# First loads in another order, the values of two blocks in one set of transfers, the first weights in four transfers, and the scales of expert 0's weights from sums of absolutes on ACT

## The chip, the core and the metric

The kernel runs on one core of one Trainium2 chip. The metric is the device time of one execution in microseconds (us): the kernel before took 1921.61 us, the median of three runs (1919.76 to 1923.17). The profile is that of one execution which took 1919.81 us. Its span, from the first to the last instruction, is 1917.9 us, so 1.9 us of that execution lie around the span.

## The reference

Chunked attention with memory tokens gives a 3072 x 512 matrix. A mixture of eight experts works on it, and each expert's output is weighted by a doubly normalised matrix P.

```python
# attention: B=4, H=8, S=768, D=64; chunks of 32, context 16 left and 8 right, 8 memory tokens
for c in range(S // 32):
    k_full = concat(mem_k, k[:, :, max(0, 32*c - 16) : min(S, 32*c + 40)])
    v_full = concat(mem_v, v[:, :, same rows])
    a = softmax(q[:, :, 32*c : 32*c + 32] @ k_full.T / 8)
    out[:, :, 32*c : 32*c + 32] = a @ v_full
x = out.transpose(0, 2, 1, 3).reshape(3072, 512)
# experts: w_gate 512x8, w1 8x512x1024, w2 8x1024x512
P = exp(x @ w_gate - max); 8 times: rows of P to sum 1, columns of P to sum 1, P *= 3072 / 8
for e in range(8):
    y += P[:, e:e+1] * (relu(x @ w1[e]) @ w2[e])
```

## The kernel before

The tokens are cut into 24 blocks of 128 (six for each of the four batch entries) and into six units of 512 (four blocks), each made of two groups of 256. The attention makes a block at a time. Queries, keys and "extra" keys (`kx`: the keys after the block, and the memory keys) are loaded and turned on TensorE (`tq`, `tk`, `tx`), the scores (`sp`) are made in 64 small matmuls, VectorE takes the maximum and subtracts it, ScalarE takes the exponential, the weights are turned (`ta`), multiplied with the values (`xp`), divided by their sum (`rec`, `xq`) and turned into a column layout (`xt`, copied to `xg`).

The experts' matmuls are done in 16-bit pairs: a 32-bit operand is multiplied by a power of two, its upper part is rounded to 16 bits on ScalarE (line 513), and VectorE takes the rest (line 521). Three products of the parts stand for one 32-bit product. The power of two for an operand is found from its largest absolute value (`scales`, line 434): a maximum along each partition, a transpose of the 128 maxima on TensorE (`row_x`, `row_w`), a maximum of these, a bit mask that leaves the exponent, a matmul that spreads the result over the partitions (`sp_x`, `sp_w`), and a reciprocal. For the values of the attention the maxima of `v` serve as a bound of its output: `vmax` (line 974) is found for each of the first four blocks, of blocks 0 and 1 for the first group's scale, and of all four for the first unit's.

Expert 0 on the first unit is made as plain products, so that it can begin early: `pp` (line 2045) are its first layer's products for one group of 256 tokens, `yp` (line 2126) its second layer's. They need expert 0's `w1` in four pieces (`w1f`, loaded by lines 543 to 553 and split by `plain1`), its `w2` in four pieces (`w2f`, split by `plain2`), and the two scales. All later products (`px`, `py`, `pz`, `yx`, `yy`, `yz`, line 1598) use a seven-product scheme for 2 x 2 blocks.

The program is not written in the order in which it runs. Every step is a task with an engine, a cost, what it depends on and a priority, and `Plan.run` (line 164) plays the tasks against these costs and hands out the instructions of each engine in that order. Where the plan finds TensorE without work for more than 0.4 us, it lays filling matmuls there (`warm`, line 427), which compute nothing that is used. The order is fixed when the program is built: on the chip each engine takes its instructions in that order and waits where an input is missing. Loads and stores are issued by SP (SyncE's queue), some of the first by ACT (ScalarE's queue). The framework gives every transfer one of eight semaphores in turn (called DMAHW0 to 7 in the program), and a transfer is not issued before the transfer eight places earlier has landed.

The names and lines for what follows: `load_block` (q and k of a block), `load_extra` (kx), `load_values` with `go_v` (line 921, eight transfers of 56 KB for a block), `go_m` and `copy_m0` (lines 890 and 908, the memory values and their copies within the on-chip memory), `take_m` (line 913, the copy of finished value buffers on POOL for the next blocks), `load` and `most` (lines 549, 551 and 558), `fetch_first` and `first_hidden`. Of the ACT queue's order at the start one has to know that the value loads of line 921 stand on it ahead of ScalarE's first computation.

Of the kernel before, what the change touches and what calls it, by code (L numbers as in the profile page):

```python
# [23 lines left out]
ISSUE = 0.5  # L24
BEHIND = 5.0
FIRST = 2.0
MARGIN = 8.0
APART = 3.6
# [3 lines left out]
class Task:  # L32


    __slots__ = ("eng", "cost", "fn", "prio", "left", "ready", "end", "then", "takes", "frees", "n", "dma", "start", "many")
# [55 lines left out]
class Plan:  # L91
# [14 lines left out]
    def add(self, eng, cost, fn, deps=(), prio=0.0, bufs=(), takes=None, frees=None, dma=0.0, many=False):  # L106
# [3 lines left out]
        t.many = many  # L110
        if dma:
            t.cost = cost * ISSUE
# [51 lines left out]
    def run(self):  # L164
        clock = {e: 0.0 for e in self.ENGINES}
        waiting = {e: [] for e in self.ENGINES}
        able = {e: [] for e in self.ENGINES}
        dma = FIRST
# [4 lines left out]
        while left:  # L173
# [45 lines left out]
            for s in t.then:  # L219
# [14 lines left out]
def tile_chunked_attn_sinkhorn_moe(  # L234
# [83 lines left out]
    ones = one.broadcast_to([P, P])  # L318
    idle = ident.bitcast(BF16)
# [114 lines left out]
    def scales(part, s, u, name, deps, prio, pool=None):  # L434
# [20 lines left out]
        def inverse(a):  # L455
            nc.vector.tensor_scalar_mul(u, a, 2.0**-SHIFT)
# [74 lines left out]
    w1v = w1.rearrange("e (kt p) (fh fp f) -> e fp p kt fh f", p=P, fh=2, fp=FP)  # L531
    w2v = w2.rearrange("e (fh fp p) d -> e fp p fh d", fh=2, fp=FP)
# [3 lines left out]
    def load(e, fp, which, prio, ahead="", eng="SP", after=()):  # L536
        shape = [P, 2, KT, P] if which == 1 else [P, 2, DM]
# [8 lines left out]
        def go():  # L546
            if which == 1:
                for fh in range(2):
                    queue.dma_start(st.t[:, fh], w1v[e, fp, :, :, fh])
# [3 lines left out]
        return st, add(eng, 2 if which == 1 else 1, go, after, prio, [st], dma=2.1)  # L553

    def most(e, fp, which, st, deps, prio):
        def go():
            flat = st.t.rearrange("p a k f -> p (a k f)" if which == 1 else "p a d -> p (a d)")
# [10 lines left out]
    def scale_w(e, which, deps, prio, pool=None):  # L568
# [9 lines left out]
            pool,  # L578
        )
# [14 lines left out]
    def cut(e, fp, which, st, ld, prio):  # L594
# [12 lines left out]
        if which == 1:  # L607
            a11, a12 = lambda: st.t[:, 0, 0:2], lambda: st.t[:, 0, 2:4]
            a21, a22 = lambda: st.t[:, 1, 0:2], lambda: st.t[:, 1, 2:4]
# [25 lines left out]
        if which == 1:  # L635
# [3 lines left out]
                    lambda: st.t[:, 0],  # L639
# [21 lines left out]
        else:  # L661
            pieces = [(slice(2, 3), slice(0, 1), (0.5, 0.65)), (slice(4, 7), slice(1, 4), (0.9, 1.1))]
# [1665 lines left out]
```

## Time and profile before

| | us |
|---|---|
| median of three runs | 1921.61 |
| the profiled execution | 1919.81 |
| its span | 1917.9 |
| TensorE (PE) busy | 1903.2 |
| VectorE (DVE) busy | 1436.4 |
| ScalarE (ACT) busy | 1033.6 |
| GpSimd (POOL) busy | 524.4 |

TensorE is busy in nearly the whole span, and what counts is therefore how much of this is work that has to be done. A row of the stretches has the stretch, its length, the busy time of each engine with its number of instructions, the granted clock (1.00 is full), the DMA engines' busy share (it can come out over 1) and the rate in GB/s. A row of the timeline has a start, a length, the engine, line, operation, what it writes and reads, the number of instructions merged, and in brackets how long the engine had been idle and what ended that. SPq and ACTq are the two queues that issue transfers.

### The profile page before, as it was taken

Reading aid. Unit: us, or ns where it says so; the run is one execution under the profiler, and the core shown is the slowest. Engines: PE = TensorE matmul, PEld = TensorE weight load, DVE = VectorE, ACT = ScalarE, POOL = GpSimd, SP = SyncE. Lnnn points to the kernel's source line nnn. Section 1 sums busy time; section 2 is a strip of 40 time slices with the busy share of each in tenths; the row PEclk is TensorE's granted clock in tenths of the full one; section 3 lists DMA queues with packets and bytes.
Section 4 is the critical chain, followed back from the end, with each engine's and each line's share of the span. In section 5 each row is a group of like instructions: output and inputs, shape, how many; then the busy total and the mean of one; then the engine's idle time right before and its main releaser. Section 6 shows DMA issues by size and latency. Waiting matters only on the chain.

```text
span 1917.9 us, 47295 instructions
## 1 busy us (share of the span) xinstructions
PE 1903.2 (99%) x19616; PEld 1641.0 (86%) x19616; DVE 1436.4 (75%) x2396; ACT 1033.6 (54%) x2019; POOL 524.4 (27%) x549
## 2 busy tenths in 40 slices
PE   9999999999999999999999999999999999999999
PEld 7777676688888888888888888888888888888888
DVE  6776569778679866898668875898678885786565
ACT  4765565556456545646445554655555554564453
POOL 1220001544224221432124231342124232332112
PEclk9999999999999999999999999999999999999999
DMA  8678753453235342265214533245313732322321
GB/s 198 174 194 209 171 172 116 129 204 125 83 110 172 127 148 85 78 197 185 92 63 149 197 105 127 78 160 176 138 45 105 242 122 94 100 83 84 127 83 67
DMA packets 246791, 254.82 MB, mean 133 GB/s; under 512 B 113264, under 2 KB 180272, under 8 KB 242224
## 3 DMA queue, kind: packets, MB, share of 16 engines
q1 hardware_dynamic: 244452, 251.21, 41.2%
q8 instruction: 153, 2.51, 0.6%
q10 hardware_dynamic: 2124, 0.59, 0.2%
q14 instruction: 62, 0.51, 0.1%
HBM read 187.84 MB, written 63.44 MB: 131 GB/s over the span
## 4 chain that ended last, share of the span: by engine, by line
PE 96%; DMA 2%; DVE 1%; ACT 0%; issue 0%; SPq 0%; ACTq 0%; DVEq 0%
PE px L1598 26%; PE yx L1598 23%; PE pz L1598 13%; PE yz L1598 11%; PE py L1598 6%; PE yp L2126 6%; PE yy L1598 6%; DMA q<-in_q_dram 1%; PE xp L1137 1%; PE sp L1069 1%; PE pp L2045 1%; PE tq L1006 1%; PE tk L1010 0%; PE ta L1127 0%; PE xt L1178 0%; DVE w L521 0%
## 5 line engine op out<-in xcount | busy, mean ns | idle before, releaser
L1598 PEld LDWEIGHTS <-w 128*128 128x128 f16 x7896 | 771.4, 98 | 91.9 <-issue 0.6
L1598 PEld LDWEIGHTS <-h 128*128 128x128 f16 x7056 | 690.4, 98 | 81.4 <-issue 1.5
L1598 PE MATMUL px<-x,w 128*128 128x256 f16 x4512 | 549.1, 273 | 0.0
L1931 POOL TENSOR_TENSOR acc<-acc,y 128x256 f32<-128x256 f32 x252 | 267.5, 1068 | 862.1 <-ACT y L1906 842.7
L1598 PE MATMUL yx<-w,h 128*128 128x256 f16 x4032 | 467.5, 273 | 1.3 <-DVE acc L1941 1.3
L1657 ACT ACTIVATE q<-px 128x256 f32<-128x256 f32 x376 | 142.8, 381 | 294.2 <-PE px L1598 289.5
L1598 PE MATMUL pz<-x,w 128*128 128x256 f16 x2256 | 278.2, 273 | 0.0
L1598 PE MATMUL yz<-w,h 128*128 128x256 f16 x2016 | 233.8, 273 | 0.0
L1826 DVE TENSOR_TENSOR h<-ss,h 128x1024 f16<-128x1024 f32 x160 | 215.0, 1346 | 4.0 <-ACT h L1802 3.5
L1777 ACT ACTIVATE h<-c 128x768 f16<-128x768 f32 x168 | 140.8, 838 | 106.4 <-DVE c L1667 106.4
L1802 ACT CAST h<-ss 128x1024 f16<-128x1024 f32 x168 | 174.1, 1039 | 20.4 <-DVE ss L1766 19.6
L1766 DVE SCALAR_TENSOR_TENSOR ss<-c,ss 128x256 f32<-128x256 f32 x336 | 168.3, 501 | 8.2
L1810 DVE SCALAR_TENSOR_TENSOR h<-c,h 128x768 f16<-128x768 f32 x168 | 165.3, 984 | 9.2 <-ACT h L1777 9.1
L1667 DVE SCALAR_TENSOR_TENSOR c<-px,q 128x256 f32<-128x256 f32 x188 | 78.0, 422 | 103.2 <-PE px L1598 94.9
L1906 ACT ACTIVATE y<-yx,pscale 128x256 f32<-128x256 f32 x168 | 79.4, 473 | 114.8 <-PE yx L1598 110.6
L1598 PE MATMUL py<-x,w 128*128 128x256 f16 x1128 | 139.2, 273 | 0.0
L2126 PE MATMUL yp<-w,h 128*128 128x512 f16 x576 | 132.0, 379 | 0.0
L1667 DVE SCALAR_TENSOR_TENSOR c<-py,q 128x256 f32<-128x256 f32 x188 | 78.5, 422 | 60.2 <-PE py L1598 56.7
L1766 DVE SCALAR_TENSOR_TENSOR ss<-c,h 128x512 f32<-128x512 f32 x168 | 120.8, 719 | 3.1 <-ACT h L1754 3.0
L1598 PE MATMUL yy<-w,h 128*128 128x256 f16 x1008 | 116.9, 273 | 0.0
L2126 PEld LDWEIGHTS <-h 128*128 128x128 f16 x576 | 56.0, 98 | 57.9
L513 ACT ACTIVATE w<-ws,sw 128x1024 f16<-128x1024 f32 (+1 forms) x64 | 69.3, 1089 | 65.5 <-POOL ws L602 65.5
(158 smaller groups left out, 1773.0 us busy)
## 6 DMA issues: line engine op xcount, KB each, us to landing
x<-xkeep SPq DMA_DIRECT2D x28, 1792.0 KB
akeep<-acc SPq DMA_DIRECT2D x168, 256.0 KB
acc<-akeep SPq DMA_DIRECT2D x168, 256.0 KB
w1f<-in_moe_w_dram SPq DMA_DIRECT2D x72, 256.0 KB
w2f<-in_moe_w_dram SPq DMA_DIRECT2D x32, 512.0 KB
w1fm<-in_moe_w_dram SPq DMA_DIRECT2D x56, 256.0 KB
w2fm<-in_moe_w_dram SPq DMA_DIRECT2D x28, 512.0 KB
xkeep<-x SPq DMA_DIRECT2D x6, 1792.0 KB
```

What stands on the lines that cost most here:

```text
L513: lambda: nc.scalar.activation(dst(0), src(), AF.Copy, scale=s),
L1598: nc.tensor.matmul(dst.t, a, b, start=(not more and n == 0), stop=(n == end), skip_group_check=more,)
L1657: lambda: nc.scalar.activation(t.t, src.t, AF.Copy, scale=DOWN),
L1667: lambda: nc.vector.scalar_tensor_tensor(c.t[:, o], src.t, DOWN, q.t, op0=ALU.mult, op1=ALU.add),
L1766: lambda: nc.vector.scalar_tensor_tensor(dst(), src(), 0.0, other(), op0=ALU.max, op1=op),
L1777: lambda: nc.scalar.activation(h.t[:, 0, 0:3], c.t, AF.Relu),
L1802: lambda: nc.scalar.copy(h.t[:, 0, 3:7], ss.t),
L1810: lambda: nc.vector.scalar_tensor_tensor(h.t[:, 1, 0:3].rearrange("p a n -> p (a n)"), c.t.rearrange("p a n -> p (a n)"), 0.0, h.t[:, 0, 0 ...
L1826: lambda: spare.tensor_tensor(h.t[:, 1, 3:7], ss.t, h.t[:, 0, 3:7], op=ALU.subtract),
L1906: (lambda: nc.scalar.activation(t.t, src.t, AF.Copy, scale=f))
L1931: lambda: nc.gpsimd.tensor_tensor(acc.t[:, cols], acc.t[:, cols], q.t, op=ALU.add),
L2126: nc.tensor.matmul(py.t, hf.t[:, hl, where[fh], o : o + P], room(fp, WIDE * wl + DM * fh, WIDE * wl + DM * (fh + 1)), start=(fp == 0 and i ...
```

## The change

The costs in the plan are altered (a transfer takes a lane out of eight, loads are given other durations, ACT begins after a table load), and with them parts of the order of the whole program. The first block's first 16 rows of k and v, which are masked, are set to zero on POOL and no longer loaded. The values of blocks 0 and 1 are loaded together by one function, all from SP. `w1` is cut so that a piece is one transfer with rows of 1 KB, where it was two with rows of 512 bytes. For expert 0 the largest absolute value of a weight piece on DVE (`most`) gives way to the sum of absolutes on ACT (`total`), with a shift larger by two. A one-column exponential at the start has ACT load its table there.

```diff
-ISSUE = 0.5
-BEHIND = 5.0
-FIRST = 2.0
+ISSUE = 0.45
+LANES = 8
+BEFORE = 0.7
+TABLE = 2.2
+BEGIN = 1.0
+AFTER = 1.2
+LATER = 1.0
...
-APART = 3.6
+APART = 2.5
...
             if t.dma:
-                at = max(at, dma - BEHIND)
-                t.start = at
-                clock[t.eng] = at + t.cost
-                dma = max(dma, at + t.cost / 2) + t.dma
-                t.end = max(dma, at + t.cost) + 2.6
+                t.start = max(at, lanes[0])
+                for _ in range(t.count):
+                    at = max(at, lanes.pop(0))
+                    dma = max(dma, at + BEGIN) + t.dma / t.count
+                    lanes.append(dma + AFTER)
+                    at += ISSUE
+                clock[t.eng] = at
+                t.end = dma + AFTER
...
-                    late = MARGIN if s.prio - t.end > FAR else 0.0
+                    late = MARGIN if s.prio - t.end > FAR else LATER if s.eng == "PE" else 0.0
...
+    first = misc.tile([P, 1], F32, name="first")
+    nc.scalar.activation(first, one, AF.Exp)
...
-    w1v = w1.rearrange("e (kt p) (fh fp f) -> e fp p kt fh f", p=P, fh=2, fp=FP)
-    w2v = w2.rearrange("e (fh fp p) d -> e fp p fh d", fh=2, fp=FP)
+    w1v = w1.rearrange("e (kt p) (fp f) -> e fp p kt f", p=P, fp=FP)
+    w2v = w2.rearrange("e (fp fh p) d -> e fp p fh d", fh=2, fp=FP)
...
-                for fh in range(2):
-                    queue.dma_start(st.t[:, fh], w1v[e, fp, :, :, fh])
+                queue.dma_start(st.t.rearrange("p k a f -> p k (a f)"), w1v[e, fp])
...
-        return st, add(eng, 2 if which == 1 else 1, go, after, prio, [st], dma=2.1)
+        return st, add(eng, 1, go, after, prio, [st], dma=1.45 if which == 1 else 1.35)
...
+    def total(e, fp, which, st, deps, prio):
+        def go():
+            nc.scalar.activation(
+                room(0, 0, 1024),
+                st.t.rearrange("p k a f -> p (k a f)" if which == 1 else "p a d -> p (a d)"),
+                AF.Abs,
+                accum_out=mxs[:, e, which - 1, fp : fp + 1],
+            )
+
+        return add("ACT", 1.2, go, deps, prio, [st, first2[0]])
...
-    BLOCKS = (-50.0, -44.0, -30.0, -26.0)
+    BLOCKS = (-50.0, -49.0, -30.0, -26.0)
...
+        if n == 0:
+            ks.append(add("POOL", 0.2, lambda: nc.gpsimd.memset(kt.t[0:LC], 0.0), (), at, [kt]))
...
+        def go_both(queue):
+            for par in range(2):
+                p0 = par * KW
+                if par == 0:
+                    for o in range(2):
+                        queue.dma_start(
+                            vt.t[o * KW + LC : o * KW + WIN, 0, :, 0:D],
+                            v[0, o::2, 0 : CH + RC].rearrange("h t d -> t h d"),
+                        )
+                whole = v_pair[p0 : p0 + WIN].rearrange("p n c h d -> p (n c) h d")
+                for i in range(HP):
+                    at = v[0, 2 * i + par, CH - LC : CH - LC + WIN]
+                    at = replace(at, ap=[at.ap[0], [CH * D, 2 * CB - 1], at.ap[1]])
+                    queue.dma_start(whole[:, 1:, i, 0:D], at)
...
+            if n == 0:
+                lv = [
+                    add("SP", 2 + 2 * HP, lambda: go_both(nc.sync), (), at, [vt], dma=4.2),
+                    add("POOL", 0.2, clear, (), at, [vt]),
+                ]
+            elif n == 1:
+                lv = list(vs[0][1])
...
-                dma=7.0,
+                dma=4.3,
...
-            found.append(most(0, fp, which, st, [ld], at - 12.0))
-        scale_w(0, which, found, at - 10.0, "att")
+            found.append(total(0, fp, which, st, [ld], at - 12.0))
+        scale_w(0, which, found, at - 10.0, "att", SHIFT + 2)
```

The `dma=7.0` stands at the store of a unit's operands (`xkeep`) and at its load; `dma=1.3` of the accumulators' stores and loads becomes 0.7.

The first place is the start of SP's queue, from the extra keys on. Before, with q of block 1 behind the first block's values:

```order
L790 DMA kx_175<-in_k_dram 32x8x64
L921 DMA v_pair<-in_v_dram 16x4x64
L921 DMA v_pair<-in_v_dram 40x4x64
L921 DMA v_pair<-in_v_dram 56x4x64 x3
L848 DMA q_188<-in_q_dram 128x8x64
L845 DMA k_192<-in_k_dram 128x8x64
L790 DMA kx_175<-in_k_dram 32x8x64 x2
L921 DMA v_pair<-in_v_dram 56x4x64 x4
L549 DMA w1f_0_286<-in_moe_w_dram 128x4x128 x2
L549 DMA w1f_1_334<-in_moe_w_dram 128x4x128 x2
L549 DMA w1f_2_341<-in_moe_w_dram 128x4x128 x2
L549 DMA w1f_3_376<-in_moe_w_dram 128x4x128 x2
```

The same place in the changed kernel:

```order
L823 DMA kx_172<-in_k_dram 32x8x64
L880 DMA q_178<-in_q_dram 128x8x64
L877 DMA k_180<-in_k_dram 128x8x64
L823 DMA kx_172<-in_k_dram 32x8x64 x2
L959 DMA v_pair<-in_v_dram 40x4x64 x2
L967 DMA v_pair<-in_v_dram 56x7x64 x8
L943 DMA v_pair<-v_pair 8x7x260 x2
L560 DMA w1f_0_325<-in_moe_w_dram 128x4x256
L560 DMA w1f_1_327<-in_moe_w_dram 128x4x256
L560 DMA w1f_2_330<-in_moe_w_dram 128x4x256
L560 DMA w1f_3_332<-in_moe_w_dram 128x4x256
```

Block 1's q and k have moved ahead of all values; the copies of the memory values have come over from ACT and stand ahead of the weights.

The second place is ACT. Its first rows before:

```order
L890 DMA v_pair<-in_mem_v_dram 8x4x64 x2
L921 DMA v_pair<-in_v_dram 16x4x64
L921 DMA v_pair<-in_v_dram 40x4x64
L921 DMA v_pair<-in_v_dram 56x4x64 x7
L908 DMA v_pair<-v_pair 8x7x260 x2
L1034 ACT_TABLE_LOAD
L1034 ACTIVATE qT_245<-tq_239 128x512
```

And the rows of the changed kernel's ACT from the values' weights of block 0 (`at`) to the first split of the weights (line 525). In the kernel before, the four rows of line 581 stood on DVE as maxima (line 558):

```order
L1209 COPY at_388<-ta_344 128x512
L1082 COPY kC<-kxT_249 128x4x24
L581 ACTIVATE w_0_0_434,mxs<-w1f_0_325 128x1024
L1171 ACTIVATE s_436<-s_436 128x512
L581 ACTIVATE w_0_0_434,mxs<-w1f_1_327 128x1024
L1247 COPY xg_476<-xt_465 128x4x128
L1209 COPY at_481<-ta_471 128x512
L581 ACTIVATE w_0_0_434,mxs<-w1f_2_330 128x1024
L581 ACTIVATE w_0_0_434,mxs<-w1f_3_332 128x1024
L1093 ACTIVATE qT_562<-tq_547 128x512
L1247 COPY xg_476<-xt_557 128x4x128
L525 ACTIVATE x_575<-xg_476,sx 128x512 x2
```

The changed kernel's ACT begins with the table load, the one-column exponential and the two memory loads, and then computes; block 1's exponential (`s_436`) now stands behind the first sum of absolutes.

The third place is SP's queue around the first piece of w2. Before:

```order
L921 DMA w_0_3_386<-in_v_dram 56x4x64 x8
L551 DMA w2f_0_652<-in_moe_w_dram 128x2x512
L551 DMA w2f_1_655<-in_moe_w_dram 128x2x512
L848 DMA q_659<-in_q_dram 128x8x64
L551 DMA w2f_2_706<-in_moe_w_dram 128x2x512
L551 DMA w2f_3_751<-in_moe_w_dram 128x2x512
L845 DMA k_786<-in_k_dram 128x8x64
```

Now (`w_0_2` and `w_0_3` are the value buffers of blocks 2 and 3, q_702 is q of block 4, as q_659 was):

```order
L562 DMA w2f_0_432<-in_moe_w_dram 128x2x512
L975 DMA w_0_2_353<-in_v_dram 56x4x64 x8
L975 DMA w_0_3_438<-in_v_dram 56x4x64 x8
L562 DMA w2f_1_681<-in_moe_w_dram 128x2x512
L562 DMA w2f_2_683<-in_moe_w_dram 128x2x512
L562 DMA w2f_3_692<-in_moe_w_dram 128x2x512
L880 DMA q_702<-in_q_dram 128x8x64
L877 DMA k_707<-in_k_dram 128x8x64
```

Three pieces of w2 now stand ahead of block 4's q, where two stood. On PE the number of filling matmuls goes from 168 to 106. Before, 157 of them (44 at the very start) stand ahead of the first `pp` product and 11 behind it; in the changed kernel all 106 (31 at the start) stand ahead of it. From the first `pp` to the turning of block 4's q (`tq`), PE then has this to do: 54 `pp` products before, 60 now, each time with the scores of blocks 2 and 3 and the turns that go with them.

More of the change, by code (lines that the diff above doesn't have):

```diff
@@ L23 @@
 HSHIFT = 18
[L24 to L26 removed]
+ISSUE = 0.45
[5 more added lines that the diff above has]
+LATER = 1.0
 MARGIN = 8.0
[L28 removed]
+APART = 2.5
 FAR = 60.0
 class Task:
[L35 removed]
+    __slots__ = ("eng", "cost", "fn", "prio", "left", "ready", "end", "then", "takes", "frees", "n", "dma", "start", "many", "count")
 class Past:
@@ L110, in add @@
         t.many = many
+        t.count = cost
         if dma:
```

127 lines of the change are left out of this document (73 added, 54 removed).

## The prediction

> **What bounds the kernel now.** I read the stretches first: a stretch, its length, the busy time of PE, PEld, DVE, ACT and POOL, the granted clock, the DMA share and GB/s.
>
> ```profile
> 0.00:33.30 33.30, 29.49 (x467) 24.13 (x468) 16.66 (x35) 14.01 (x26) 4.95 (x12) 1.00 0.81 182
> 33.30:70.00 36.70, 34.73 (x688) 26.19 (x686) 33.24 (x56) 28.05 (x52) 5.33 (x5) 1.00 0.73 169
> 70.00:500.00 430.00, 424.22 (x5509) 322.92 (x5508) 304.39 (x561) 246.52 (x492) 111.09 (x113) 1.00 0.57 165
> 500.00:1500.00 1000.00, 1000.00 (x9162) 896.26 (x9161) 789.56 (x1264) 541.86 (x1054) 303.21 (x317) 1.00 0.38 129
> 1500.00:1918.00 418.00, 414.72 (x3799) 371.46 (x3797) 292.51 (x485) 203.20 (x400) 99.86 (x103) 1.00 0.30 102
> ```
>
> TensorE is the bound from 70 us on, and a full one from 500 to 1500. But the filling matmuls count as busy. The same stretches (and two at the very start) for the fills alone:
>
> ```profile
> 0.00:33.30 33.30, 20.46 (x157) 1.00 0.81 182
> 33.30:70.00 36.70, 0.74 (x6) 1.00 0.73 169
> 70.00:300.00 230.00, 1.20 (x8) 1.00 0.69 183
> 1.56:4.50 2.94, 2.94 (x14) 1.00 0.73 164
> 4.50:8.10 3.60, 3.60 (x32) 1.00 0.87 162
> ```
>
> So PE's time that computes nothing, idle plus fills, is 3.81 + 20.46 = 24.3 us up to 33.3, 1.97 + 0.74 = 2.7 us up to 70, 5.78 + 1.20 = 7.0 us up to 500, and 3.3 us after 1500, at the end. PE's real work (1903.2 - 22.4 = 1880.8 us) is the same after the change. **The change can only move this waste of 37 us**, and two thirds of it lie ahead of the first `pp`. What holds `pp` back, from the timeline:
>
> ```profile
> 1.56 6.54 PE L427 MATMUL warm<-ident 128*128 128x256 bf16 x44 [1.56 <-POOL ident masks.py:199]
> 1.67 5.77 ACTq L921 DMA_DIRECT2D v_pair<-in_v_dram  x9
> 9.14 1.28 ACT L1034 ACT_TABLE_LOAD   x1 [9.14 <-DMA v_pair<-in_v_dram]
> 7.95 0.60 PE L1006 MATMUL tq<-ident,q 128*128 128x128 f32 x4
> 10.93 0.71 ACT L1014 COPY kC<-tk 128x672 f32<-128x672 f32 x1
> 12.64 0.86 PE L1069 MATMUL sp<-kC,qT 64*32 64x64 f32 x64 [0.22 <-ACT kC L1027]
> 15.94 5.81 SPq L549 DMA_DIRECT2D w1f<-in_moe_w_dram  x8
> 21.72 2.34 DVE L558 TENSOR_REDUCE mxs<-w1f 128x1 f32<-128x1024 f32 x2
> 26.36 1.21 DVE L558 TENSOR_REDUCE mxs<-w1f 128x1 f32<-128x1024 f32 x1
> 29.09 1.33 ACT L513 ACTIVATE x<-xg,sx 128x512 f16<-128x512 f32 x2 [0.42 <-DVE sx L457]
> 30.70 0.16 DVE L457 RECIPROCAL sw<-uw 128x1 f32<-128x1 f32 x1
> 30.93 3.23 ACT L513 ACTIVATE w<-w1f,sw 128x1024 f16<-128x1024 f32 x3
> 31.44 1.22 DVE L974 TENSOR_REDUCE vmax<-w 128x1 f32<-128x1024 f32 x1
> 32.58 3.67 DVE L521 SCALAR_TENSOR_TENSOR w<-w1f,sw,w 128x1024 f16<-128x1024 f32 x3
> 33.38 1.14 PE L2045 MATMUL pp<-x,w 128*128 128x256 f16 x6
> ```
>
> Three things are late one after the other. ACT issues value loads until 9.1 and loads its table only then, though `tq` was through by 8.6. The weights' loads begin at 15.9. The fourth maximum stands behind the attention on DVE and starts at 26.4; scale, split and first product follow from there.
>
> **The change, part by part.**
>
> *ACT freed at the start.* The nine value loads, the two copies and the 1.28 us of table load leave ACT's path: it is free from about 3 us. PE is next: its 31 fills, 14 of them in 2.94 us and 17 at 3.60/30 = 0.12 (44 - 14 = 30 in the row up to 8.10), end at 6.5, so `tq` runs at 6.5, `tk` after four fills at about 7.4, `kC` from 8.0 instead of 10.93. The distance from `kC` to `sp` was 1.7 us, so block 0's scores start at 9.8 instead of 12.64: 2.9 us earlier. The memsets on POOL hide behind the loads.
>
> *Loads.* The rates:
>
> ```profile
> 0.00:10.00 10.00, 8.44 (x63) 7.08 (x64) 0.14 (x2) 0.86 (x1) 0.91 (x8) 1.00 0.61 120
> 10.00:16.00 6.00, 5.21 (x103) 4.02 (x102) 2.34 (x4) 3.57 (x10) 2.82 (x3) 1.00 0.98 182
> 16.00:24.00 8.00, 7.16 (x190) 5.75 (x197) 6.01 (x10) 4.18 (x9) 1.22 (x2) 1.00 0.94 265
> 38.00:44.00 6.00, 6.00 (x113) 5.29 (x111) 5.97 (x8) 4.01 (x10) 0.00 (x0) 1.00 1.10 359
> 0.73 0.45 SPq L848 DMA_DIRECT2D q<-in_q_dram  x1
> 4.11 0.35 SPq L782 DMA_DIRECT2D kx<-in_k_dram  x1
> SPq L782 <- DMA q<-in_q_dram: 1.8, 1, 1.8
> ```
>
> Rows of 256 bytes (q, k, v) move at 182/0.98 to 120/0.61, 186 to 197 GB/s; the weights, in rows of 512 bytes before, at about 282 when the engines are full (265/0.94), and w2 with its longer rows at 326 to 359. The first 10 us were used to 0.61 only: small transfers waited for one of eight places: kx, until 4.11, for the place of q. q had thus landed 3.4 us after its issue at 0.73, of which its 0.26 MB are 1.3; I put 1.2 ahead of a load's first byte and 0.9 behind its last (an estimate from these). Now the first eight places hold 0.90 MB, not 0.66. Ahead of w1 stand 2.18 MB in short rows (q, k 1.02, kx 0.26, values 0.89, memory 0.02): 11.2 us at 195 GB/s, from 0.7 + 1.2 = 1.9 on, is 13.1, and the copies 0.3 more. The 2.10 MB of w1 take 6.4 us at 330 (5.8 at 359, 7.4 at 282): the last byte at 19.8, landed about 20.6 (18.8 to 22.5), the first piece at 15.6. Before, the issue alone lasted until 21.75.
>
> *Sums on ACT for maxima on DVE.* The trace has no sum of absolutes. Nearest is ACT's split of the same tile, 1.1 us each (3.23 for three); reading the sum out may take an instruction of its own, for which I allow 0.4, over half of `kC`'s 0.71. I take 1.2, with 1.0 and 1.5 as ends. A maximum on DVE was 1.21. The wait that it adds: behind the first sum stand block 1's exponential, `xg` and `at`. So exponential 16.8 to 17.4, second sum 18.6, `xg` and `at` 19.8, third and fourth sum 22.2. Meanwhile `xp` of block 1, its division and turn follow `at` by 2.8 us (0.9, 1.1, 0.65 and lags) and are ready at 22.6.
>
> *From the last sum to `pp`.* ACT has qT, `xg`, the two `x` and a `kC` ahead of the weights, 0.6 + 0.6 + 1.25 + 0.6 = 3.05 us (0.71 of a copy and 1.33 of two splits, each less its 0.1 of overlap): 25.25. The scale took 3.3 us from the last maximum (26.36 + 1.21) to the reciprocal (30.70 + 0.16), 0.5 of it behind other work on DVE, so it comes at about 25.1 and hides there. Split on ACT 1.15, on DVE 1.28 (no `vmax` of another block in between: that of 31.44 ended at 32.66, 0.6 us after the first piece was through ACT): **`pp` at 27.7 instead of 33.3, -5.6 us**. PE's queue allows it: 14 fills in 2.94, 92 at (20.46 - 2.94)/143 = 0.1225, 9.0 us of real work, from 1.6 on, is 24.8. With the ends of loads and sums it is 26.2 to 29.5.
>
> *After `pp`.* Here the cover goes. Ahead of block 4's q now stand three w2 pieces and the values of blocks 2 and 3, and values go out slowly:
>
> ```profile
> 24.08 5.50 SPq L921 DMA_DIRECT2D w<-in_v_dram  x8
> 30.79 4.06 SPq L921 DMA_DIRECT2D w<-in_v_dram  x8
> 42.70 0.60 PE L1006 MATMUL tq<-ident,q 128*128 128x128 f32 x4
> PE tq L1006 <- DMA q<-in_q_dram: 2.4, 3, 1.1
> PE xp L1137 <- issue: 2.5, 2, 1.7
> ```
>
> PE wanted q of block 4 at 42.70, 9.3 us behind the first `pp`. Six more products (0.65) and a transpose of 128 maxima (0.2) now stand between: 10.2 us, so at 37.9. The loads: 0.5 to 0.7 us for each transfer of 56 KB is under the engines' rate. q and k of blocks 2 and 3 (1.05 MB) last until 25.2, w2's first piece until 26.7, the values, whose places come free one by one, until about 32; three pieces at 340 take 4.6 us, q 1.3, landing 0.9: q lands at 38.0 to 39.6. PE waits 0.1 to 1.7 us, where it had not waited; block 4's k and kx come as closely behind, and I take the upper end, 1.5 in all. ACT has four more sums there (4.8 us) and DVE four maxima less (4.8): DVE, the fuller of the two in the second stretch (33.24 of 36.70, ACT 28.05), is relieved, and ACT comes to 32.9, about where DVE was. Its lateness falls into the same wait. Up to 70 I set 3.4 us of waste against 2.7, as the wait is new and the six fills go: **+0.7** (-1.7 to +5). From 70 to 500 the eight fills go, with half of their 1.2 us turning into idle time: **-0.6** (-2.5 to +2.5). w1's halved number of transfers and the later loads hide under PE.
>
> A rule that speaks against taking fills away: the Trainium skill, "TensorE: Matmul & The Clock Gate", section "What's actually happening", has PE at half clock until about 3.4 us of activity, and again after an idle window of as much. The trace agrees on the first part by its rate (0.21 us a fill for 2.94 us, then 0.12) though the granted clock shows 1.00; the longest wait of PE behind the first `pp` is the 1.7 us above, too short for the second, and by the forecast none here is longer than 3.
>
> *Sum:* -5.6 + 0.7 - 0.6 = -5.5 us: 1914.3 for an execution like the profiled 1919.81. That one lies 1.8 under the median of the runs; taken from the median 1921.61 it is **1916.1**.
>
> **The rivals.**
>
> *The stream of loads is the bound after `pp`* (15%). If each value load takes 0.69 us to issue, as the 5.50 row, not 0.45 to 0.5, 16 of them put q of block 4 back by 3.8 us, and PE waits 5.3: -5.5 + 3.8 = -1.7, 1919.9. For it: PE waited for q three times, and DVE was 33.24 of 36.70 busy, so little slack is about. Against: the 4.06 row.
>
> *w1 lands no earlier* (8%), since rate and not order holds it: landed at 24, last sum at 25.5, `pp` at 31: -2.3 + 0.7 - 0.6 = -2.2, 1919.4. Against: 0.61 in the first 10 us.
>
> *The clock falls back* (7%): a wait of over about 3 us for q of block 4, then 3 us at half rate as in the row of the 14 fills: 1.5 us more, beside 1.6 more of waiting: -5.5 + 3.1 = -2.4, 1919.2. No idle time in this trace is long enough to show it. It is the case of the gate rule of the Trainium skill's page "TensorE: Matmul & The Clock Gate" above, at this place.
>
> *Slower: the stores of the units' operands* (8%).
>
> ```profile
> 78.32 0.60 SPq L1256 DMA_DIRECT2D xkeep<-x  x1
> 79.01 10.05 DMA q<-in_q_dram
> 83.00:84.00 1.00, 1.00 (x28) 0.82 (x11) 0.86 (x3) 1.00 (x3) 0.00 (x0) 1.00 1.05 442
> ```
>
> A q load issued right behind the first store took 10 us. The plan now books 4.3 us for a store instead of 7.0, so it may call for the q behind each of the six stores 2.7 us sooner than it comes. Four such stalls are 10.8 us: -5.5 + 10.8 = +5.3, 1926.9. It makes the kernel slower from three stalls (8.1) on, and by over 0.2% from four. Against: 1.835 MB at 442 GB/s are 4.2 us, so the new figure is the truer one.
>
> **How the numbers follow.** The forecast has 62%. All ends on one side would be -7.1 - 1.7 - 2.5 = -11.3 (1910.3) and -3.8 + 5 + 2.5 = +3.7 (1925.3); they seldom fall together, and I cut 1 in 10 off on each side, the stores' case with it: 1911 to 1922.5. 0.2%, about what a measurement of this kernel tells from no change, is 3.8 us. Nine tenths of the forecast's 62% lie beyond it (0.56), and a little of the clock's case: faster 0.58. What is left of these two, w1 and the stream: same 0.34. The stores: slower 0.08.
>
> **What would show it.** Right: the table load at 1 us, `sp` of block 0 near 10, SP done with w1's issue by 14, the fourth sum ending near 22, `pp` near 28, no fills behind it, and a wait of `tq` for q of 0 to 3 us before 45. Wrong: sums of 1.5 us or more, a `pp` after 30, waits for q over 4 us, or idle time in the stretch of 70 to 500 over 9 us; and any idle time from 500 to 1500, where I expect none.

## The result, and the profile after

| | before | after |
|---|---|---|
| median, us (4 runs each, on one chip) | 1920.88 | 1940.64 |
| lowest to highest | 1919.76 to 1923.17 | 1939.22 to 1942.90 |
| ratio to before, 95% interval | | 1.0103 (1.0090 to 1.0115) |
| the profiled execution, its span | 1919.81, 1917.9 | 1940.67, 1938.9 |

The change made the kernel **slower by 19.8 us**, where 5.5 us faster had been forecast; the range ended at 1922.5. The profiled spans differ by 21.0 us. The stretches of the kernel after (stretch, length, busy time of PE, PEld, DVE, ACT, POOL, granted clock, DMA share, GB/s):

```profile
0.00:33.30 33.30, 26.85 (x423) 20.83 (x424) 12.40 (x31) 18.95 (x35) 6.03 (x15) 1.00 1.02 199
33.30:70.00 36.70, 33.09 (x610) 25.15 (x609) 25.25 (x45) 28.21 (x56) 4.42 (x5) 0.95 0.68 156
70.00:500.00 430.00, 421.10 (x5499) 317.71 (x5498) 303.44 (x563) 244.31 (x487) 107.82 (x113) 0.99 0.55 160
500.00:1500.00 1000.00, 991.05 (x9058) 885.48 (x9057) 769.10 (x1242) 531.56 (x1036) 298.67 (x307) 1.00 0.37 125
```

And the fills alone, in the first of them:

```profile
0.00:33.30 33.30, 15.57 (x106) 11.21 (x106) 1.00 1.02 199
```

Two things stand out. PE, without a gap from 500 to 1500 before, is now idle for 8.95 us there and has done 9058 matmuls instead of 9162; at the 1.31 us in which 12 of them follow one another (the starts 382.53 and 383.84 further down are of such neighbours) the 104 are 11.4 us. And the granted clock, 1.00 in every stretch before, is 0.95 and 0.99 early on. Over the whole execution the page has, after:

```profile
span 1938.9 us, 47022 instructions
PE 1906.1 (98%) x19554; PEld 1637.4 (84%) x19554; DVE 1420.1 (73%) x2388; ACT 1037.9 (54%) x2036; POOL 524.2 (27%) x552
```

That is idle 1938.9 - 1906.1 = 32.8 us (14.8 before), fills 15.6 (22.4), and 1906.1 - 15.6 = 1890.5 of other work against 1880.8, 9.7 more. So 6.8 us of fills went, 18.0 of idle time came, and the same work took 9.7 longer. By stretch, idle time and fills together are 22.0 us up to 33.3 (24.3 before), 3.6 up to 70 (2.7), 8.9 up to 500 (7.0) and 8.95 from 500 to 1500 (none).

*Where it is lost.* Two kinds of matmul serve as milestones: `yp`, the second product of expert 0, and `yx`, that of all later experts. Groups by shape (line, engine, tile, count, shortest, median and longest ns, first and last start in us), before:

```profile
L2126 PE MATMUL yp<-w,h x576: 376/379/391, 55.9 to 381.3; 128*128 128x512 f16 x192
L1598 PE MATMUL yx<-w,h x4032: 269/273/273, 400.0 to 1914.4; 128*128 128x256 f16 x192
```

and after:

```profile
L2189 PE MATMUL yp<-w,h x576: 376/379/391, 57.2 to 382.3; 128*128 128x512 f16 x192
L1661 PE MATMUL yx<-w,h x4032: 269/273/273, 406.5 to 1935.2; 128*128 128x256 f16 x192
```

Expert 0 ends 1.0 us later. From its last `yp` to the first `yx` takes 24.2 us, not 18.7: 5.5 lost at the changeover. From the first to the last `yx` 1528.7, not 1514.4: 14.3 lost. These three make 20.8 of the 21.0 us, and 19.8 of them lie behind 382 us, where the loads and sums of the start have long been done.

*What it is lost to, at the changeover.* `acc` is a running sum of the experts' outputs, stored by one expert and loaded again for the next; `w1fm` is a piece of a later expert's w1, loaded for its maximum `mxs`. The timeline of the kernel after, rows of SP, ACT, DVE and PE (start, length, engine, line, what is written and read; in brackets the idle time ahead and what ended it):

```profile
383.15 0.82 SPq L1910 DMA_DIRECT2D acc<-akeep  x2
384.07 0.38 SPq L560 DMA_DIRECT2D w1fm<-in_moe_w_dram  x1
...
387.58 0.72 ACT L1920 ACTIVATE acc<-acc,pscale 128x512 f32<-128x512 f32 x1 [3.16 <-DMA acc<-akeep]
389.75 0.72 ACT L1920 ACTIVATE acc<-acc,pscale 128x512 f32<-128x512 f32 x1 [1.45 <-DMA acc<-akeep]
390.38 0.36 ACT L1720 ACTIVATE q<-px 128x256 f32<-128x256 f32 x1
...
391.12 1.22 DVE L569 TENSOR_REDUCE mxs<-w1fm 128x1 f32<-128x1024 f32 x1 [5.27 <-DMA w1fm<-in_moe_w_dram]
...
382.53 1.47 PE L1661 MATMUL px<-x,w 128*128 128x256 f16 x12
383.84 1.47 PE L1661 MATMUL py<-x,w 128*128 128x256 f16 x12
...
390.80 0.82 PE L1661 MATMUL px<-x,w 128*128 128x256 f16 x6 [2.86 <-ACT q L1720]
```

Read it from the last row up. PE waits 2.86 us for ACT to empty a product's bank (`q`). ACT had been free, but at the head of its queue stood the scaling of two reloaded sums (`acc`), which were not there: they landed 4.4 and about 6.2 us behind their issue. DVE in the same time waits 5.27 us for a tile of w1 that landed 7.05 us behind its issue, with copies of products (`c`) queued behind the maximum. The plan had called such a tile landed after 1.0 + 1.45 + 1.2 = 3.65 us and a reloaded sum after 1.0 + 0.7 + 1.2 = 2.9, on an idle stream. (The plan before: 5.2 for the two halves of a w1 piece, 4.95 for w2.)

Half clock then follows, as these rows of the stretches show:

```profile
392.00:394.00 2.00, 1.90 (x12) 1.48 (x12) 2.00 (x4) 0.60 (x3) 0.39 (x1) 0.68 0.60 150
394.00:396.00 2.00, 2.00 (x12) 1.39 (x11) 1.88 (x4) 0.84 (x1) 1.92 (x4) 0.50 0.67 252
```

*And later.* The waits of DVE and ACT from 500 to 1500 that ended with a transfer (us in sum, times, longest), after:

```profile
DVE mxs L569 <- DMA w1fm<-in_moe_w_dram: 17.3, 8, 3.7
DVE mxs L569 <- DMA w2fm<-in_moe_w_dram: 5.6, 3, 2.7
ACT acc L1920 <- DMA acc<-akeep: 4.9, 4, 1.7
```

and before:

```profile
DVE mxs L558 <- DMA w2fm<-in_moe_w_dram: 1.9, 2, 1.1
```

DVE is busy for 769 of these 1000 us and far from a bound; but its queue is worked off in order. A maximum whose tile is late holds up the copies behind it, and PE finds no free bank a little later. One instance in the timeline after:

```profile
839.05 0.38 SPq L560 DMA_DIRECT2D w1fm<-in_moe_w_dram  x1
...
845.39 1.22 DVE L569 TENSOR_REDUCE mxs<-w1fm 128x1 f32<-128x1024 f32 x1 [1.49 <-DMA w1fm<-in_moe_w_dram]
...
852.60 1.47 PE L1661 MATMUL px<-x,w 128*128 128x256 f16 x12 [1.87 <-DVE c L1730]
```

The tile landed 6.3 us behind its issue. PE's own waits of this kind, over the whole execution after (the trace of before has none of 0.2 us or more):

```profile
PE px L1661 <- DVE c L1730: 9.9, 12, 1.9
PE px L1661 <- ACT q L1720: 5.0, 4, 2.9
```

*The start* went the forecast's way, but by less. Timeline after:

```profile
0.72 1.28 ACT L330 ACT_TABLE_LOAD   x1 [0.72 <-PEq L2381]
1.56 6.19 PE L439 MATMUL warm<-ident 128*128 128x256 bf16 x31 [1.56 <-POOL ident masks.py:199]
10.80 0.86 PE L1128 MATMUL sp<-kC,qT 64*32 64x64 f32 x64
11.70 1.60 SPq L943 DMA_DIRECT2D v_pair<-v_pair  x2
13.35 3.10 SPq L560 DMA_DIRECT2D w1f<-in_moe_w_dram  x4
17.97 1.22 DVE L1032 TENSOR_REDUCE vmax<-v_pair 128x1 f32<-128x1024 f32 x1 [4.60 <-DMA v_pair<-v_pair]
19.00 1.06 ACT L581 ACTIVATE w<-w1f 128x1024 f16<-128x1024 f32 x1 [3.10 <-DMA w1f<-in_moe_w_dram]
19.96 0.18 ACT L581 ACTIVATION_READ_ACCUMULATOR w<-w1f 128x1 f32 x1
25.49 0.19 ACT L581 ACTIVATION_READ_ACCUMULATOR w<-w1f 128x1 f32 x1
28.87 3.34 PE L439 MATMUL warm<-ident 128*128 128x256 bf16 x29
32.05 0.38 PE L2108 MATMUL pp<-x,w 128*128 128x256 f16 x2
44.51 1.06 PE L1065 MATMUL tq<-ident,q 128*128 128x128 f32 x4 [1.97 <-DMA q<-in_q_dram]
```

### The profile page after: what moved, and what is told of

Same layout as the page of the kernel before. It is cut to its first block, busy times and chain, and to the rows that moved or that the text cites. A ratio compares the mean times of both kernels' runs of the same rounds, so it can differ in the third digit from the quotient of the medians.

```text
span 1938.9 us, 47022 instructions
## 1 busy us (share of the span) xinstructions
PE 1906.1 (98%) x19554; PEld 1637.4 (84%) x19554; DVE 1420.1 (73%) x2388; ACT 1037.9 (54%) x2036; POOL 524.2 (27%) x552
## 4 chain that ended last, share of the span: by engine, by line
PE 87%; DMA 6%; DVE 4%; issue 1%; SPq 1%; ACT 0%; POOL 0%; DVEq 0%; ACTq 0%; POOLq 0%
PE px L1661 22%; PE yx L1661 22%; PE yz L1661 11%; PE pz L1661 11%; PE yp L2189 6%; PE yy L1661 6%; PE py L1661 6%; DMA w1fm<-in_moe_w_dram 1%; DVE ss L1829 1%; DMA akeep<-acc 1%; DVE w L533 1%; PE xp L1200 1%; DMA q<-in_q_dram 1%; PE sp L1128 1%; DMA acc<-akeep 1%
## 5 line engine op out<-in xcount | busy, mean ns | idle before, releaser
L1889 DVE TENSOR_TENSOR h<-ss,h 128x1024 f16<-128x1024 f32 x160 | 210.4, 1316 | 4.1 <-ACT h L1865 4.1
L1829 DVE SCALAR_TENSOR_TENSOR ss<-c,ss 128x256 f32<-128x256 f32 x336 | 174.0, 518 | 8.3
```

The lines of the kernel that those rows point to most:

```text
L1829: lambda: nc.vector.scalar_tensor_tensor(dst(), src(), 0.0, other(), op0=ALU.max, op1=op),
L1889: lambda: spare.tensor_tensor(h.t[:, 1, 3:7], ss.t, h.t[:, 0, 3:7], op=ALU.subtract),
```

## The experiments

Theory A, formed from these rows: the plan's new figures (shorter transfers, and a landing 1.2 us behind the last byte) put instructions that read a late load too early into DVE's and ACT's queues, and everything behind 382 us is lost to that. Its rivals: the new loads and sums of the start cost the time (theory B), or the stores' booking (the rival on record). All of the medians below stand beside 21 to 33 runs of the kernel before on the same chip.

| run | median, us | ratio to before (95%) | last `yp` | first to last `yx` | DVE waiting for `w1fm`, 500 to 1500 |
|---|---|---|---|---|---|
| e1, old booking, rest new | 1920.28 | 0.9993 (0.9983 to 1.0002) | 380.2 | 1516.2 | 0 |
| e2, new booking, rest old | 1945.61 | 1.0123 (1.0104 to 1.0143) | 392.2 | 1526.6 | 16.5 |
| e3, e1 with maxima on DVE | 1918.46 | 0.9988 (0.9979 to 0.9997) | 377.1 | 1516.4 | 0 |
| e4, late transfers land 5.0 behind | 1917.74 | 0.9980 (0.9971 to 0.9990) | 378.1 | 1514.0 | 0 |
| e5, so for weights only | 1922.76 | 1.0014 (1.0005 to 1.0024) | 381.3 | 1517.1 | 0 |
| e6, so for all but weights | 1933.52 | 1.0077 (1.0062 to 1.0092) | 379.5 | 1528.4 | 9.3 |
| e7, e4 and 24 fills ahead of a wait | 1919.74 | 1.0000 (0.9991 to 1.0008) | 380.6 | 1514.8 | 0 |
| e9, stores booked at 7.0 | 1939.85 | 1.0104 (1.0090 to 1.0117) | 382.0 | 1530.0 | 17.0 |
| e10, e4 with block 4's q ahead of w2 | 1922.75 | 1.0013 (1.0004 to 1.0022) | 382.5 | 1514.5 | 0 |
| e11, old durations, new landing | 1919.85 | 0.9995 (0.9986 to 1.0004) | 378.7 | 1515.4 | 0 |
| e12, new durations, landing 2.6 | 1918.42 | 0.9985 (0.9976 to 0.9994) | 379.1 | 1514.9 | 4.6 |
| e13, e4 with w1's maxima on DVE | 1919.85 | 0.9995 (0.9986 to 1.0003) | 380.7 | 1514.8 | 0 |

**e1 and e2: each half alone.** e1 is the kernel after with every hunk of the plan turned back: figures of `dma=`, places, landing, `APART`. Loads, w1's layout and sums stay new. Its core:

```diff
-                t.start = max(at, lanes[0])
-                for _ in range(t.count):
...
-                t.end = dma + AFTER
+                at = max(at, dma - BEHIND)
+                t.start = at
+                clock[t.eng] = at + t.cost
+                dma = max(dma, at + t.cost / 2) + t.dma
+                t.end = max(dma, at + t.cost) + 2.6
```

> The changed kernel with the plan's booking of transfers as it was before (one shared DMA clock, 2.6 us to landing, the old durations, APART 3.6); new order of the first loads, one transfer per piece of w1 and the sums of absolutes on ACT stay. Theory A (the new booking calls a load landed too soon, so that DVE and ACT stand before loads and PE behind them): no PE idle time to speak of from 500 to 1500, and 1912 to 1921 us. Theory B (the sums on ACT, the longer single transfers of w1 or the new first loads cost the time): 1935 us or more, with the waits of px for DVE still there.

e2 is the mirror image: the kernel before with those hunks alone.

> The kernel before with the new booking of transfers alone (lanes, 1.2 us to landing, the shorter durations, APART 2.5); its loads, layouts and maxima on DVE stay. Theory A: 1935 to 1945 us, with 8 us or more of PE idle time from 500 to 1500 and DVE's maxima waiting for w1fm or w2fm. Theory B: within 4 us of before, 1917 to 1925.

The row from 500 to 1500 of e1:

```profile
500.00:1500.00 1000.00, 999.52 (x9157) 895.00 (x9156) 789.84 (x1262) 541.52 (x1054) 300.29 (x316) 1.00 0.37 129
```

and of e2:

```profile
500.00:1500.00 1000.00, 993.15 (x9085) 888.59 (x9084) 765.88 (x1241) 532.21 (x1037) 294.89 (x307) 1.00 0.38 125
```

e1 is the kernel before to within the interval, with 0.48 us idle in this stretch; e2 is slower by 24 us, with 6.85 idle. Theory B falls: what is lost comes with the booking and goes with it. e2 also loses at the start (its last `yp` is at 392.2, 10.9 us later than before), which the kernel after does not: there the new loads do gain something against the new booking.

**e3: sums or maxima, under the old booking.** e1 with `most` in place of `total` and the old shift.

```diff
-            found.append(total(0, fp, which, st, [ld], at - 12.0))
+            found.append(most(0, fp, which, st, [ld], at - 12.0))
```

> As the run with the old booking, and the maxima of expert 0's weights back on DVE: the new first loads, the table load and the one transfer per piece of w1 alone. Theory A: 1914 to 1922 us, and the difference to the run with the sums on ACT is what these are worth (1 to 4 us in the first 35 us). Theory B, if the sums are to blame: faster than that run by 8 us or more.

The intervals of e1 and e3 overlap: there the sums on ACT gain nothing that could be told (the first `pp` came at 34.6 in e1's profile and at 33.4 in e3's). The new loads with the old booking and old maxima gain 0.12% (0.03 to 0.21).

**e4: only the landing, and only late.** The kernel after, with transfers called landed 5.0 us behind their bytes once the filling has ended (the orders of the two programs part at about 300 us; up to there all engines do the same in the same order).

```diff
-                t.end = dma + AFTER
+                t.end = dma + (AFTER if self.fill is not None else 5.0)
```

> The changed kernel, with a transfer booked as landed 5.0 us behind its last byte instead of 1.2 once the fills have ended (from about 430 us on). Theory A: the 9 us of PE idle time from 500 to 1500 shrink to 3 or less and the time falls to 1927 to 1933 us; the first 400 us stay as they are. Theory B: no change, 1938 to 1943.

1917.74 against the 1940.64 of after: one figure takes the whole loss back, and more of it than was expected. It has also **the lowest ratio of all the kernels here** (with an interval that overlaps those of e3 and e12), and is faster than before by 0.20% (0.10 to 0.29). Its milestones:

```profile
L2189 PE MATMUL yp<-w,h x576: 376/379/390, 57.0 to 378.1; 128*128 128x512 f16 x192
L1661 PE MATMUL yx<-w,h x4032: 272/273/273, 396.7 to 1910.7; 128*128 128x256 f16 x192
```

18.6 us at the changeover and 1514.0 behind it, as before (18.7 and 1514.4). PE's own order is the same in both programs from the first row to the last; only the others' differ. Here DVE's queue at the wait of 5.27 us, in the kernel after:

```
497 L1730 SCALAR_TENSOR_TENSOR c_5_3_6297<-py_5_3_6280,q_1_5_3_6277 128x256
498 L569 TENSOR_REDUCE mxs<-w1fm_2_6244 128x1
499 L533 SCALAR_TENSOR_TENSOR w_1_3_6232<-ws_1_3_6254,sw,w_1_3_6232 128x1024
500 L1730 SCALAR_TENSOR_TENSOR c_5_2_6288<-px_5_2_6246,q_1_5_2_6339 128x256
501 L1730 SCALAR_TENSOR_TENSOR c_5_3_6297<-px_5_3_6258,q_1_5_3_6347 128x256
502 L1730 SCALAR_TENSOR_TENSOR c_5_2_6288<-pz_5_2_6309,q_1_5_2_6306 128x256
```

and in e4, where the maximum of the same tile stands behind the copies:

```
496 L1730 SCALAR_TENSOR_TENSOR c_5_3_6290<-py_5_3_6272,q_1_5_3_6270 128x256
497 L569 TENSOR_REDUCE mxs<-w2fm_1_6210 128x1
498 L533 SCALAR_TENSOR_TENSOR w_1_3_6226<-ws_1_3_6247,sw,w_1_3_6226 128x1024
499 L1730 SCALAR_TENSOR_TENSOR c_5_2_6279<-px_5_2_6239,q_1_5_2_6331 128x256
500 L1730 SCALAR_TENSOR_TENSOR c_5_3_6290<-px_5_3_6251,q_1_5_3_6340 128x256
501 L1730 SCALAR_TENSOR_TENSOR c_5_2_6279<-pz_5_2_6304,q_1_5_2_6301 128x256
502 L1730 SCALAR_TENSOR_TENSOR c_5_3_6290<-pz_5_3_6316,q_1_5_3_6311 128x256
503 L569 TENSOR_REDUCE mxs<-w1fm_2_6235 128x1
```

The maximum has moved by four copies and a split of weights, and nothing waits for it.

**e5 and e6: which loads.** e5 applies e4's line to weights alone, e6 to all other transfers.

```diff
-                t.end = dma + AFTER
+                t.end = dma + (5.0 if self.fill is None and t.late else AFTER)
```

> The changed kernel, in whose plan only the loads of weights, and only from the point where the filling ends (about 380 us), are called landed 5.0 us behind their bytes instead of 1.2; attention rows, values and the reloaded sums keep 1.2. Theory A1 (the later weights' loads are called landed too early, so a maximum on VectorE stands at the head of its queue before its tile is there, and the copies of products behind it come late): all or nearly all of the 21 us comes back, 1917 to 1923, idle time from 500 to 1500 under 2 us. Theory A2 (every kind of late load has its part, the reloaded sums waited for 20 us by ScalarE too): about half, 1926 to 1934, 4 to 6 us idle from 500 to 1500. If neither (the gain of the run with all loads late came from another order of work): over 1936.

> The complement: all loads and stores but the weights are called landed 5.0 us behind their bytes from about 380 us on, the weights keep 1.2. A1: no better than the changed kernel, 1936 to 1943, VectorE still waiting some 17 us for first weights from 500 to 1500. A2: 1928 to 1936. If neither: as the changed kernel or slower.

The kernel after, e4 and this pair were timed on different occasions, so the ratios are compared: e4 takes back 1.23% of the time before, e5 0.89 and e6 0.26. The weights are the larger part, and they are most of what is lost behind the changeover: first to last `yx` is 1517.1 with them mended (1514.0 in e4), 1528.4 without. At the changeover either is enough: it takes 18.6 us in e5 (381.3 to 399.9) and 19.0 in e6 (379.5 to 398.5), against 24.2. So the 5.5 us lost there are not the reloaded sums' alone, nor the weights' alone. e6's total is lower than theory A1 had it, so neither theory held alone.

**e9: the rival on record.** The kernel after with the stores of the units' operands booked at 7.0 us again.

```diff
-                dma=4.3,
+                dma=7.0,
```

> The changed kernel with one figure of the plan put back: the six stores of the units' operands are booked at 7.0 us again, not 4.3. The rival of the prediction (loads of q called behind a store sooner than they come, four stalls, 10.8 us): 1928 to 1935. Theory A (the loss sits behind 380 us, where no such store is): within 3 us of the changed kernel, 1937 to 1944, idle time from 500 to 1500 still 7 us or more.

1939.85: that rival falls. The loss was not made by a q that stalls behind a store.

**e11 and e12: durations or landing.** e11 puts back the old `dma=` figures of all transfers and keeps the places and the 1.2; e12 keeps the figures and has late transfers land 2.6 us behind.

```diff
-                t.end = dma + AFTER
+                t.end = dma + (AFTER if self.fill is not None else 2.6)
```

> The changed kernel with the plan's old durations of transfers (weights 2.1 us, q and k 1.55, values 1.35 and 5.4, stores 7.0, sums 1.3), while its eight places and its landing 1.2 us behind the last byte stay. If the shorter durations make the loss: 1919 to 1926. If the earlier landing makes it (2.6 before, and up to 5 us of queue ahead): 1934 to 1942. Both a part: between.

> The changed kernel with the landing of late loads called 2.6 us behind the last byte, as the plan before had it, not 1.2 or 5.0; durations and places new. If the 1.4 us taken from the landing are the cause: 1918 to 1924. If 1.2 to 5.0 works by steps (a tile is asked for by the next free place in the queue): 1926 to 1935. If durations are the cause: 1933 to 1941.

Either alone takes the whole loss back. So neither figure is the cause by itself; the two together leave too little. A w1 tile counts as there after 3.65 us in the kernel after, 4.3 in e11, 5.05 in e12 and 7.45 in e4, on an idle stream. Only the first loses; a DVE that waits 4.6 us in sum, as in e12, or 6.1 for w2 in e11, still costs PE nothing that can be seen (rows from 500 to 1500, e12 and then e11):

```profile
DVE mxs L569 <- DMA w1fm<-in_moe_w_dram: 4.6, 6, 1.4
```

```profile
DVE mxs L569 <- DMA w2fm<-in_moe_w_dram: 6.1, 4, 1.9
```

The longest single waits are 1.4 and 1.9 us there, and 2.8 to 3.7 in the four kernels (after, e2, e6, e9) that wait 9 to 17 us in sum and lose 12 to 16 us from the first to the last `yx`: so in these kernels waits of 1 to 2 us were covered, and those of about 3 were not. The sum alone does not tell: e6 waits 9.3 us for w1 and loses 14.0, the kernel after 17.3 and 14.3.

**e7: is the half clock a cost of its own?** e4 waits 3.22 us for q of block 4 at 43.7 and then runs at half clock until 50. e7 issues 24 fills right ahead of these transposes, into the bank that they are to write.

```diff
         def go_q():
+            if n == 4:
+                wp = tq.t[:, 0:2].rearrange("p h d -> p (h d)")
+                for _ in range(24):
+                    nc.tensor.matmul(wp, idle[:, 0:P], idle, start=True, stop=True)
```

> The run with all late loads called landed later (1917.7), and 24 filling matmuls (about 2.6 us) issued on TensorE right ahead of block 4's transposes of q, where that run waited 3.2 us and then ran at half clock for some 4 us. Theory C (the half clock behind the wait is a cost of its own, about 2 us, and filling the wait avoids it): granted clock 1.00 from 33 to 70, idle ahead of tq under 1 us, 1914.5 to 1917.0. Rival (time is set by when q and the loads behind it land, a slow TensorE only waits less later): 1917.2 to 1919.5.

Timeline of e7, PE:

```profile
40.81 2.78 PE L1067 MATMUL tq<-ident 128*128 128x256 bf16 x24
44.40 0.66 PE L1069 MATMUL tq<-ident,q 128*128 128x128 f32 x4 [0.80 <-DMA q<-in_q_dram]
...
53.69 0.63 PE L1069 MATMUL tq<-ident,q 128*128 128x128 f32 x4 [1.49 <-DVE w L533]
```

The clock stayed full behind the filled wait (0.66 us for the transposes, 1.09 in e4), and the time did not improve: at 53.69 TensorE waited 1.49 us (0.46 at the same place in e4), and 56 to 58 ran at half clock instead. Theory C falls; by the ratios e7 is if anything slower than e4, and its median lies 0.2 us above the rival's range. That the bytes and the splits set the time there, as the rival has it, fits these rows but was not tested alone.

**e10: is the wait itself?** e4, with three pieces of w2 made to wait for q and k of block 4.

```diff
+        if n == 4:
+            for t in w2first:
+                t.left += 2
+                lq.then.append(t)
+                lk.then.append(t)
```

> The run with all late loads called landed later (1917.7), in which three pieces of w2 are loaded behind q, k and the values of block 4, not ahead of them. Theory D (PE's wait of 3.2 us for q of block 4 is a loss of its own, made by the three w2 pieces ahead of it): no wait of tq over 1 us before 45, granted clock 1.00 from 33 to 70, 1913.5 to 1916.5. Rival (the stretch is set by the bytes that it needs, w2 with them: the wait moves to w2's sums, scale or first product): 1917 to 1920, a wait behind w2 of 2 us or more.

No wait for q is left before 54, and PE waits for w2's scale instead (timeline of e10):

```profile
53.56 0.27 PE L507 MATMUL row_w<-ident,most_of 128*1 128x128 f32 x1 [3.20 <-DVE most_of L458]
```

It is slower than e4. In its queue the extra keys and the values of block 4 go out ahead of w2 as well, and the three pieces are issued from 43.35 on, not from 34.92 as in e4. The wait moved.

**e13: sums or maxima, under the new booking.** e4, with w1's maxima on DVE and w2's sums on ACT.

> The run with all late loads called landed later (1917.7), in which the scales of the first w1 come from maxima on VectorE again, as before, and only those of w2 from sums on ScalarE. Theory E (four sums of 1.2 us on ScalarE gain nothing at w1, as the loads of the copies and of w1 set the time and ScalarE has block 1's exponential and xg between them): 1916 to 1919, first pp within 1 us of 29.9 to 32. Rival (the sums bring the first product forward, as the prediction had it): pp 2 us or more later and 1919 to 1922.

Its first `pp` comes at 34.1, that of the five executions that share the kernel after's start at 29.9 to 32.05. So here the sums seem to bring the first product forward, by 2 to 4 us, though e13 gives one execution only and under the old booking it was the other way (34.6 in e1, 33.4 in e3). Of the total little is left: 1919.85 against 1917.74, measured on different occasions, with intervals of the ratios that overlap. With e3 beside it, their worth stays open within some 2 us either way.

## Why the prediction was wrong

**The step that failed** is the last of its working, one sentence: "w1's halved number of transfers and the later loads hide under PE", with "any idle time from 500 to 1500, where I expect none" as its test. What came there was 8.95 us of idle time, and 19.8 us of loss behind 382 us in all. The step took the new `dma=` figures and the landing for a change to the order of the start. They are the plan's clock for 1938 us of program, and the order of DVE's queue follows from it up to the end. DVE at 79% and PE at 100% of the stretch before do not say that there is room: the order, not the load, kept each maximum behind its tile. The signs were in the traces of before: DVE waited there already for w2's tiles, 1.9 us of it from 500 to 1500.

**The ledger** ("the change can only move this waste of 37 us") was wrong too, on both sides. Waste can be made where none was: 8.95 us of it from 500 to 1500, and 48.4 in all instead of 37. And the busy time of the same matmuls was not the same: 9.7 us more. Three stretches of 3.4 us at half clock (at 44.5, 256.2 and 392.7) make at most 5.1 of them; where the rest comes from no run here shows.

**The rivals.** The one on the slower side had the right kind of cause, a plan that calls a load landed before it is, at the wrong place: loads of q behind stores, during the attention, not weights and reloaded sums from the changeover on. e9 shows that its figure had no part. "Against: the new figure is the truer one" was the wrong question: 4.3 us is what the bytes take, and 3.65 may be near what one tile takes alone; a booking has to hold for a tile behind others. By the fit in the Trainium skill, "DMA: Bandwidth & Descriptors", section "Anatomy of one DMA — SWDGE (gpsimd) path", a transfer takes 2.0 us and its bytes at 436 GB/s, 3.2 us for 512 KB by my working (an estimate for one alone, on another issue path); the trace shows 6.3 and 7.05 behind others. "The clock falls back" was right in kind: it fell after a wait of 1.97, not of 3. Its place was right too, but e7 gained nothing by keeping the clock up there.

**The start, step by step.**

- *ACT freed.* Right: the table load stands at 0.72, and `sp` of block 0 at 10.80 (9.8 forecast, 12.64 before). The missing microsecond is in the 31 fills, 6.19 us where I had 5.0.
- *Loads.* The last issue of w1 was over at 16.45, not by 14, and the first piece was read at 19.00, not 15.6. The copies, set at 0.3 us, are the term that was most mis-sized: issued from 11.70 on, their 57 KB each had landed by 17.9 only, and w1 was issued behind them. That they held w1 up is argued from this order; no run took them away.
- *Sums on ACT.* Right: 1.06 and 0.18 for the accumulator, at a distance of 1.2 where the last two follow one another. The fourth ends at 25.68 (22.2 forecast), late by what w1 was late.
- *The first `pp`.* 32.05 in this execution, 29.9 to 30.8 in four others with the same start; forecast 27.7, with 26.2 to 29.5 as ends. Of the 5.6 us 1.3 to 3.5 were gained.
- *The wait for q of block 4.* There as forecast, 1.97 us (2.4 to 3.4 in the others) against 0.1 to 1.7. By the order shown ahead of the prediction four pieces of w2 stand before this q, not three as the text there says; the sum of the loads has all four. How much of `pp`'s gain it takes back is not shown: of 3.5 us in e4 3.2 are left at the last `yp` (378.1, 381.3 before), though e4 waits 3.22 for this q; 2.2 of 2.9 are left in e12, 1.8 of 2.6 in e6, and none in e5 (381.3) and the kernel after (382.3). These last two alone have another stretch at half clock near 255 us, behind waits of 2.55 and 1.95 for an exponential.

So the start, forecast at -5.5, is worth -3.4 us in the best kernel (e4) and less in its neighbours. Its mechanisms were right in the main and its sizes too large.

## What to carry to other kernels

Where a planner's figures are changed, look for what they move in the whole program, not at the place for which they were tuned: compare the order of each queue at its end too. A booking that is true for a lone transfer is too short in a queue of them; what it must cover is the latest landing that an in-order engine would have to stand and wait for, and here some 1 us more for a weight tile at either of two places (0.65 in e11, whose other durations went back too, 1.4 in e12) was worth 20. A wait on an engine that is a quarter idle costs nothing only as long as nothing that the bound engine needs is queued behind it.

## What was unexpected in the hardware

*The clock falls after waits of 2 us, but not after each.* These rows of the kernel after surround the wait of 1.97 us that ends at 44.51:

```profile
43.00:44.00 1.00, 0.00 (x0) 0.00 (x0) 0.00 (x0) 0.89 (x4) 0.00 (x0) 1.00 0.73 142
44.00:45.00 1.00, 0.49 (x3) 0.53 (x4) 0.00 (x0) 0.88 (x2) 0.00 (x0) 0.77 0.68 147
45.00:46.00 1.00, 1.00 (x5) 0.66 (x3) 0.00 (x0) 0.40 (x1) 0.00 (x0) 0.50 0.61 108
47.00:48.00 1.00, 1.00 (x18) 0.83 (x5) 0.69 (x3) 0.00 (x0) 0.00 (x0) 0.52 0.07 11
48.00:49.00 1.00, 1.00 (x10) 0.76 (x8) 0.93 (x5) 0.80 (x2) 0.00 (x0) 1.00 0.51 116
```

Some 3.4 us at half clock follow a wait of 1.97 us; a wait of 1.95 at 255.68 did the same (0.54 and 0.60 in the two stretches of 2 us behind it), while one of 1.87 at 852.60 left the clock at 1.00. So did a longer one, of 2.22 us in e2:

```profile
1527.31 1.47 PE L1608 MATMUL px<-x,w 128*128 128x256 f16 x12 [2.22 <-DVE c L1677]
1529.00:1531.00 2.00, 2.00 (x20) 1.79 (x19) 1.97 (x4) 1.83 (x6) 0.32 (x1) 1.00 0.01 2
```

The length of the wait is thus not all. In the kernel after, the three stretches at half clock begin at 44.55, 256.18 and 392.71 and last 3.41 us each, and the starts lie 62 and 40 times 3.41 us apart: the clock changes on a fixed grid. The slots of 3.41 us that end there hold 1.97, 1.95 and 2.0 us of idle time; the 2.22 us in e2 lie across a border of its grid (from the falls at 21.39, 48.70 and 137.44), with 1.58 in the one slot. That some 2 us idle within one slot bring the fall is a reading of these rows, not tested; two falls had less ahead of them (1.43 at 17.39 in e10, 1.78 at 46.29 in e5). The Trainium skill, "TensorE: Matmul & The Clock Gate", section "What's actually happening", puts the fall behind an idle window of about 3.4 us; here 1.97 us of idle time were enough.

*The same start is not the same twice.* Five kernels whose engines all do the same in the same order up to about 300 us, and PE up to the end (after, e4, e5, e6, e12), have their first `pp` at 29.9 to 32.05 and their last `yp`, by when some of the other engines' orders differ, at 378.1 to 382.3. One profile is too little for an edit of 2 us at the start.
